# Local and global attention with a gated feed-forward: 224 own key columns a block, probabilities normalised in place

## Chip, core and metric

The kernel runs on one core of a Trainium2 chip. The metric is device time in microseconds, the median of several runs. TensorE (PE in the profile) multiplies, and its weight loads (PEld) overlap the multiplication; VectorE is DVE, ScalarE is ACT, GpSimd is POOL, and SyncE (SP) issues the DMAs. SBUF is the memory on the chip, PSUM the banks that PE writes.

## What is computed

For 8 batches of 8 heads with 512 local and 32 global tokens of 64 features each:

```python
# global queries see every key
out_g = softmax(scale * q_g @ [k_g, k_l].T) @ [v_g, v_l]
# local queries see the global keys, and local keys at most 32 away
s_ll = where(abs(pos_q - pos_k) <= 32, scale * q_l @ k_l.T, -1e9)
out_l = softmax([scale * q_l @ k_g.T, s_ll]) @ [v_g, v_l]
x = [out_g, out_l] with the heads side by side     # 4352 rows of 512
out = (sigmoid(x @ w_gate) * (x @ w_val)) @ w_out   # 512 -> 1536 -> 512
```

The weights come as float64 words and all else as float32.

## The kernel before

**Precision.** A product of float32 numbers is made of float32r parts: a high part (the cast) and a low part (the number less the cast), and three products of them. So operands are split in two: ACT casts and POOL or DVE subtracts. A few heads at the start ("native") use plain float32 instead.

**Attention.** For each head the host lays q, keys and global q side by side in one row block (64 x QK, the 64 features on the partitions). The keys are a run of blocks of 160 columns (BLK): for each block j of 128 queries, a window of 224 columns (WIN) starts at column 160 j, and it holds 32 keys to the left, the first 64 own keys, the 32 global keys, the last 64 own keys and 32 to the right. Neighbouring windows share 64 columns. `load_qk` (L156) loads the row block twice, to the upper and the lower half of the partitions (`qk_raw`). `split_qk` (L187) makes `qk_hi` by a cast of all 1248 columns on ACT (L193), `kl` by a subtract of the 704 key columns on POOL (L194), and the low parts of q by two small subtracts on POOL (L196). `split_v` does the same for v: `vhl`, a cast (L205) and a subtract of 512 columns on POOL (L206).

`local_unit` (L216) treats two blocks of queries, so a head has two such units, in four stages:
- scores in `bank_x` (L225); per block, DVE adds the mask and finds the maximum into `s_sb` (L237, which the order tables call ISA), ACT takes the exponential in place and the sum (L240);
- DVE adds a small number to the sums and inverts them (L243, L244), and `scaled` (L209) multiplies the probabilities: per block one instruction for the 128 own keys (two groups of 64) and one for the 96 others (three groups of 32), from `s_sb` to `p_buf`, in the order of v's rows;
- PE transposes the four 128x128 pieces of `p_buf` into `bank_y` (L254); ACT casts them and DVE subtracts (L264) into `pt`;
- PE multiplies with v (L280, L281), ACT, DVE (L284) and POOL (L285) add the parts.

`global_unit` (L287) does the like for the 32 global queries of a head: four 256-column matmuls of scores (L299: two groups of own keys, each in high and low) and two of 32 columns (L301), a maximum (L304 to L306), an exponential (L308, L309), one scale of 32x576 in place in `pg_buf` (by `scaled`, so L213 too), five transposes (L317), and the product (L330).

**Feed-forward.** `ffn_stream` runs over chunks of 512 tokens and 12 blocks of the hidden dimension: 12 matmuls into `bank_g`, 12 into `bank_v` (L362), and, one block later, 12 of the output into `bank_o` (L396). Between them stand, for the gate, ACT (L370, L376, L377), DVE (L375 and L378, with two inputs in SBUF) and then DVE's product with the values (L380), a cast on ACT (L382) and a subtract on POOL (L383).

**Order.** Attention of the next chunk is issued between groups of four matmuls of the present one, by a table of ticks: a unit every PER = 4 ticks, its four stages 3 ticks apart, loads 16 ticks ahead, splits of q and k 10 and of v 4 ticks ahead. The framework's scheduler then sets each engine's order. Chunks 0 and 1 are half chunks of the first batch and run native, with the conversion of the weights beside them (`convert`, DVE L128 to L136, ACT L132 and L137, POOL L138); the first four heads of chunk 2 are native as well. That is the start-up, about 200 us; up to about 260 us follows the rest of chunk 2's attention, and then six whole chunks of about 139 us, all split. Which engine scales is set by the table NORM: ACT takes two of three in chunk 1 and every second one in chunk 2's native heads, DVE all others.

Of the kernel before, what the change touches and what calls it, by code (L numbers as in the profile page):

```python
# [8 lines left out]
F32 = mybir.dt.float32  # L9
# [8 lines left out]
P = 128  # L18
# [3 lines left out]
NH = 8  # L22
BLK = 160
KEXT = 4 * BLK + 64
K0 = 256
# [3 lines left out]
VS = (2, 3, 6, 7)  # L29
WIN = 224  # L30
DM = 512

# Where work is issued, in ticks of the feed-forward (one tick is four 512-token
# matmuls). Attention units of a chunk follow each other every PER ticks; a unit's
# stages lie STAGES apart, its operands are loaded and split ahead of it.
BASE, PER = 3, 4
STAGES = (0, 3, 6, 9)
LOAD_QK, LOAD_V, SPLIT_QK, SPLIT_V = 16, 9, 10, 4
LOAD_V_NATIVE = 4
# from the first of these ticks of a chunk on, attention is put off by the second  # L40
HOLE = (8, 1)
START = dict(per0=4, base1=1, per1=1.1, base2=23, per2=3, x2=28, lead=8, native_heads=4)
# [12 lines left out]
def kernel(ctx, tc, qk, v, w_gate, w_val, w_out, out_l, out_g):  # L55
# [14 lines left out]

# [1 line left out]
    ident = const.tile([P, P], F32, name="ident")  # L72
# [3 lines left out]
    nc.gpsimd.memset(masks[:, 1], 0.0)  # L76
    # window column c < 96 stands for key c - 32, c >= 128 for key c - 64
    # (relative to the block's first query); the columns between are global
    mid = masks[:, 1]
    for c0, lo, hi in ((0, 0, 64), (128, 96, -32)):  # L80
        cols = mid[:, c0:c0 + 96]
        nc.gpsimd.affine_select(out=cols, in_=cols, pattern=[[1, 96]], compare_op=ALU.is_ge, fill=NEG, base=lo,
                                channel_multiplier=-1)
        nc.gpsimd.affine_select(out=cols, in_=cols, pattern=[[-1, 96]], compare_op=ALU.is_ge, fill=NEG, base=hi,
                                channel_multiplier=1)
    for m, c0 in ((0, 0), (2, 192)):
        nc.scalar.copy(masks[:, m], mid)
        nc.gpsimd.memset(masks[:, m, c0:c0 + 32], NEG)

    p_bufs = [const.tile([P, 2, 256], F32, name="p_buf"),  # L90
              ffn.tile([P, 512], F32, name="p_first", tag="mn", bufs=1).rearrange("p (a c) -> p a c", a=2)]
    nc.vector.memset(p_bufs[0], 0.0)
    nc.vector.memset(p_bufs[1][:, :, WIN:], 0.0)
    pg = const.tile([32, 5 * P], F32, name="pg_buf")
    nc.vector.memset(pg, 0.0)
    xg32 = const.tile([P, KT, NG], F32, name="xg32")

# [53 lines left out]

# [1 line left out]
    def qcol(j):  # L153
# [62 lines left out]
    def local_unit(T, blocks, x32s, h, col0):  # L216
# [4 lines left out]
        for i, j in enumerate(blocks):  # L221
            qj = ks[0][:, qcol(j) - q0:qcol(j) - q0 + P]
            for t, (kt, k0) in enumerate(zip(ks, k0s)):
                js = slice(k0 + j * BLK, k0 + j * BLK + WIN)
                nc.tensor.matmul(s_ps[:, i, 0:WIN], qj, kt[:, js], start=t == 0, stop=t == last)  # L225
# [19 lines left out]
        for i in range(2):  # L245
            main = s_sb[:, i, 32:224].rearrange("p (a c) -> p a c", c=96)[:, :, 0:64]
            scaled(nat, pb[:, i, 0:128].rearrange("p (a c) -> p a c", c=64), main, r[:, i:i + 1])
            side = s_sb[:, i].rearrange("p (a c) -> p a c", c=32)[:, 0:7:3]
            scaled(nat, pb[:, i, 128:224].rearrange("p (a c) -> p a c", c=32), side, r[:, i:i + 1])
        yield  # L250
        pt_ps = ps.tile([P, 4, P], F32, name="bank_y", tag="att", bufs=4)
        for i in range(2):
            for t in range(2):
                nc.tensor.transpose(pt_ps[:, 2 * i + t], pb[:, i, t * P:(t + 1) * P], ident)  # L254
        if nat:
# [31 lines left out]
    def global_unit(T, b, h):  # L287
# [6 lines left out]
        sb = ps.tile([32, 32], F32, name="bank_y", tag="att", bufs=4)  # L294
        for half in range(2):
            o0 = 96 * half
            for t, (src, k0) in enumerate(zip(ks, k0s)):
                view = src[:, k0 + 32:k0 + 32 + 4 * BLK].rearrange("p (j c) -> p j c", c=BLK)[:, :, o0:o0 + 64]
                nc.tensor.matmul(sa[:, :, 64 * half:64 * half + 64], qg, view, start=t == 0, stop=t == last)  # L299
        for t, (src, k0) in enumerate(zip(ks, k0s)):  # L300
            nc.tensor.matmul(sb, qg, src[:, k0 + 96:k0 + 128], start=t == 0, stop=t == last)  # L301
        mg = small.tile([32, 4], F32, name="mg")
# [5 lines left out]
        nc.scalar.activation(pg[:, 0:512], saf, AF.Exp, bias=mg[:, 2:3], scale=0.125, accum_out=sg[:, 0:1])  # L308
# [3 lines left out]
        nc.vector.reciprocal(mg[:, 3:4], mg[:, 3:4])
        scaled(0, pg[:, 0:576], pg[:, 0:576], mg[:, 3:4])
        yield
# [23 lines left out]

# [1 line left out]
    hl_q = []  # L340
# [67 lines left out]

    # ---- driver: attention of the next chunk runs between the matmul groups
    def att_events(ci, start, per, tail=0):  # L410
        """(tick, order, thunk) of all attention work for chunk ci."""
        b, blocks, with_g = chunks[ci]
# [98 lines left out]
def host_layout(inputs):  # L511
# [11 lines left out]
    for j in range(4):  # L523
        o = 32 + j * BLK
        ke[:, o:o + 64] = kl[:, j * P:j * P + 64]
        ke[:, o + 64:o + 96] = kg
        ke[:, o + 96:o + 160] = kl[:, j * P + 64:(j + 1) * P]
# [36 lines left out]
```

## Time and profile before

| what | us |
| --- | --- |
| median of 3 runs | 1267.04 (1265.67 to 1270.59) |
| profiled execution: its span | 1265.6 |
| PE busy | 1221.5 |
| DVE busy | 877.6 |
| ACT busy | 783.3 |
| POOL busy | 570.6 |

The page gives no other time of the profiled execution than its span, from the first instruction to the last; it lies 1.4 us under the median of the runs. In the views, L254 is line 254 of the kernel before, a name like `bank_y` is a tile, x443 is a count, and an arrow names the tile read or the instruction that ended a wait.

### The profile page before, as it was taken

To read this page: it belongs to the slowest core of one execution; us is meant where nothing else is said; L and a number is where in the kernel's file an instruction comes from. 1 tells how busy PE (TensorE), PEld (TensorE's weight loads), DVE (VectorE), ACT (ScalarE), POOL (GpSimd) and SP (SyncE) were. 2 spreads that over 40 slices of the span, in tenths; PEclk is the share of its full clock that TensorE was granted. 3 is DMA by queue.
4 is the path that set the end of the run, shared out by engine and by line. 5 is a ranking of instruction groups with operands and counts; after the bars stand their busy time and mean duration, and the time that the engine had idled before them with its cause. 6 is when DMAs were issued, how large, how long until landed. Compare 5 with 4: busy or idle time off the path is not lost.

```text
span 1265.6 us, 20474 instructions
## 1 busy us (share of the span) xinstructions
PE 1221.5 (97%) x6820; PEld 994.1 (79%) x6820; DVE 877.6 (69%) x2433; ACT 783.3 (62%) x1899; POOL 570.6 (45%) x573
## 2 busy tenths in 40 slices
PE   5899989999999999999999999999999999999998
PEld 4676768788788877888788877888788877888897
DVE  4797976757877777857876778767775787632232
ACT  4586766756666666666666667756765766532233
POOL 1444554545555355545555455535554555311111
PEclk9698999999999999999999999999999999999999
DMA  5576864333333333333333423343334332122143
GB/s 198 197 259 225 254 191 145 92 121 99 92 107 98 115 99 108 91 121 108 107 92 107 126 78 107 109 127 111 92 86 126 116 92 87 44 90 67 67 133 117
DMA packets 59497, 151.90 MB, mean 120 GB/s; under 512 B 6144, under 2 KB 19456, under 8 KB 59392
## 3 DMA queue, kind: packets, MB, share of 16 engines
q1 hardware_dynamic: 59392, 150.59, 38.9%
q8 instruction: 54, 0.88, 0.3%
q14 instruction: 51, 0.42, 0.1%
HBM read 135.36 MB, written 15.20 MB: 119 GB/s over the span
## 4 chain that ended last, share of the span: by engine, by line
PE 77%; DVE 13%; ACT 5%; issue 3%; POOL 1%; DMA 1%; SPq 0%; POOLq 0%; DVEq 0%; ACTq 0%
PE bank_g L362 20%; PE bank_v L362 19%; PE bank_o L396 19%; PE bank_x L225 5%; PE bank_y L254 4%; DVE p_buf L213 3%; DVE th L378 2%; PE bank_y L317 2%; PE bank_x L330 2%; PE bank_x L280 2%; PE bank_x L299 2%; PE bank_x L281 1%; DVE pg_buf L213 1%; ACT s_sb L240 1%; DVE pt L264 1%
## 5 line engine op out<-in xcount | busy, mean ns | idle before, releaser
L362 PE MATMUL bank_g<-xt,wg 128*128 128x512 f32 (+1 forms) x1440 | 340.3, 371 | 1.8 <-DVE th L380 1.8
L362 PE MATMUL bank_v<-xt,wv 128*128 128x512 f32 (+1 forms) x1440 | 332.6, 368 | 3.0 <-DVE pt L264 2.7
L396 PE MATMUL bank_o<-wo,hh 128*128 128x512 f32 x1224 | 334.0, 404 | 0.8 <-ACT hh L382 0.4
L362 PEld LDWEIGHTS bank_g<-xt,wg 128*128 128x128 f32 x1440 | 238.6, 192 | 41.6 <-issue 3.4
L362 PEld LDWEIGHTS bank_v<-xt,wv 128*128 128x128 f32 x1440 | 237.8, 190 | 40.7 <-PE bank_y L301 3.1
L396 PEld LDWEIGHTS bank_o<-wo,hh 128*128 128x128 f32 x1224 | 214.1, 189 | 38.9 <-ACT hh L382 1.2
L383 POOL TENSOR_TENSOR hh<-th,hh 128x512 fp32r<-128x512 f32 (+1 forms) x120 | 137.6, 1147 | 199.7 <-ACT hh L382 198.8
L240 ACT ACTIVATE s_sb<-s_sb,nm 128x224 f32<-128x224 f32 x240 | 113.8, 475 | 143.1 <-DVE nm L237 142.0
L213 DVE TENSOR_SCALAR p_buf<-s_sb,r 128x128 f32<-128x128 f32 (+1 forms) x443 | 151.8, 386 | 4.2 <-PE bank_y L254 0.4
L375 DVE TENSOR_SCALAR mn<-bank_g 128x512 f32<-128x512 f32 (+1 forms) x108 | 67.3, 623 | 110.7 <-ACT th L370 109.3
L378 DVE SCALAR_TENSOR_TENSOR th<-th,mn 128x512 f32<-128x512 f32 (+1 forms) x120 | 101.5, 846 | 59.0 <-ACT mn L376 52.7
L285 POOL TENSOR_TENSOR x<-t 64x256 f32<-64x256 f32 x104 | 76.4, 734 | 142.8 <-DVE t L284 138.7
L194 POOL TENSOR_TENSOR kl<-qk_raw,qk_hi 128x704 fp32r<-128x704 f32 x52 | 88.4, 1701 | 114.8 <-ACT qk_hi L193 114.8
L370 ACT ACTIVATE th<-bank_g 128x512 f32<-128x512 f32 (+1 forms) x120 | 63.5, 529 | 97.7 <-PE bank_g L362 96.1
L382 ACT CAST hh<-th 128x512 fp32r<-128x512 f32 (+1 forms) x120 | 66.5, 554 | 68.1 <-DVE th L380 67.3
L237 DVE CUSTOM_DVE_ANT_0 s_sb<-bank_x,masks 128x224 f32<-128x224 f32 x240 | 83.8, 381 | 12.7 <-PE bank_x L225 8.4
L254 PE MATMUL bank_y<-ident,p_buf 128*128 128x128 f32 x496 | 80.1, 282 | 10.8 <-DVE p_buf L213 6.6
L196 POOL TENSOR_TENSOR qk_hi<-qk_raw,qk_hi 64x256 fp32r<-64x256 f32 x104 | 87.7, 863 | 4.1
L254 PEld LDWEIGHTS bank_y<-ident,p_buf 128*128 128x128 f32 x496 | 60.9, 143 | 32.5 <-ACT pg_buf L308 6.6
L243 DVE TENSOR_SCALAR r<-sm 128x2 f32<-128x2 f32 x128 | 29.3, 229 | 75.5 <-ACT s_sb L240 74.2
L193 ACT CAST qk_hi<-qk_raw 128x1248 fp32r<-128x1248 f32 x52 | 64.1, 1233 | 22.2 <-PE bank_y L301 22.1
L380 DVE TENSOR_TENSOR th<-bank_v,th 128x512 f32<-128x512 f32 (+1 forms) x120 | 72.4, 604 | 5.1 <-PE bank_v L362 1.3
(109 smaller groups left out, 1985.9 us busy)
## 6 DMA issues: line engine op xcount, KB each, us to landing
wo<-wo_dram SPq DMA_DIRECT2D x116, 512.0 KB, 3.5
qk_raw<-in_qk_dram SPq DMA_DIRECT2D x104, 312.0 KB, 4.4
v_raw<-in_v_dram SPq DMA_DIRECT2D x52, 256.0 KB, 2.6
out_dram<-ob SPq DMA_DIRECT2D x34, 256.0 KB, 3.0
xt<-in_w_gate_dram SPq DMA_DIRECT2D x12, 512.0 KB, 4.5
xt<-in_w_val_dram SPq DMA_DIRECT2D x12, 512.0 KB, 4.4
xt<-in_w_out_dram SPq DMA_DIRECT2D x12, 512.0 KB, 4.9
v_nat<-in_v_dram SPq DMA_DIRECT2D x8, 512.0 KB, 5.5
```

Of the source, the lines that this page charges most:

```text
L194: nc.gpsimd.tensor_tensor(kl, t[:, K0:Q1], hi[:, K0:Q1].bitcast(F32), op=ALU.subtract)
L196: nc.gpsimd.tensor_tensor(hi[64:128, r], t[64:128, r], hi[64:128, r].bitcast(F32), op=ALU.subtract)
L213: nc.vector.tensor_scalar(out, in_, by, None, op0=ALU.mult)
L237: anchor[0] = nc.vector.tensor_tensor_reduce(out=s_sb[:, i], in0=s_ps[:, i, 0:WIN], in1=masks[:, m], scale=-0.125, scalar=3.0e38, op0=ALU. ...
L240: nc.scalar.activation(s_sb[:, i], s_sb[:, i], AF.Exp, bias=nm[:, i:i + 1], scale=-1.0, accum_out=sm[:, i:i + 1])
L254: nc.tensor.transpose(pt_ps[:, 2 * i + t], pb[:, i, t * P:(t + 1) * P], ident)
L285: nc.gpsimd.tensor_tensor(dst, t0[:, :, 0], t0[:, :, 1], op=ALU.add)
L362: nc.tensor.matmul(acc, w[a][:, t, fs], xt[:, c, t, x0:x0 + ntok], start=n == 0, stop=n == 11)
L378: nc.vector.scalar_tensor_tensor(th, th, 1.0, mn, op0=ALU.add, op1=ALU.mult)
L380: nc.vector.tensor_tensor(th, acc, th, op=ALU.mult)
L383: nc.gpsimd.tensor_tensor(hh[:, 1, 0:ntok], th, hh[:, 0, 0:ntok].bitcast(F32), op=ALU.subtract)
L396: nc.tensor.matmul(o_ps[t], ph[:, a, t * P:(t + 1) * P], pwo[:, c], start=f2 == 0 and i == 0, stop=f2 == NF - 1 and i == 2)
```

## The change

Each key block now has 224 columns of its own, 128 own keys first, then 32 to the left, 32 global ones and 32 to the right; windows share nothing. A row block grows from 1248 to 1440 columns, the keys in it from 704 to 896. The two scales of a block become one 128x224 scale in place in `s_sb`, which gets two buffers; `p_buf`, `p_first` and their memsets go. The transposes read `s_sb` directly: columns 0 to 127, and 96 to 223, whose first 32 rows meet rows of zeros in v, where the side keys' rows move down by 32. The global queries' own keys are one view of four groups of 128, so two 512-column matmuls do what four did; the scale there is 32x608. The masks are made by other selects. A smaller scratch for DMA descriptors is asked for, which frees SBUF and adds no instruction. Line numbers fall by 4 to 13 (the scale L213 is L207, the transposes of L254 are L242 and L243, L264 is L253).

```diff
-BLK = 160
-KEXT = 4 * BLK + 64
+WIN = 224
+KEXT = 4 * WIN
+GC = 4 * P + 64
...
-    for c0, lo, hi in ((0, 0, 64), (128, 96, -32)):
...
+    for c0, n, step, base in ((0, P, 1, 32), (0, P, -1, 32), (P, 32, 1, 0), (192, 32, -1, -96)):
...
-    p_bufs = [const.tile([P, 2, 256], F32, name="p_buf"),
-              ffn.tile([P, 512], F32, name="p_first", tag="mn", bufs=1).rearrange("p (a c) -> p a c", a=2)]
-    nc.vector.memset(p_bufs[0], 0.0)
-    nc.vector.memset(p_bufs[1][:, :, WIN:], 0.0)
...
-                js = slice(k0 + j * BLK, k0 + j * BLK + WIN)
+                js = slice(k0 + j * WIN, k0 + (j + 1) * WIN)
                 nc.tensor.matmul(s_ps[:, i, 0:WIN], qj, kt[:, js], start=t == 0, stop=t == last)
...
-            s_sb = att.tile([P, 2, WIN], F32, name="s_sb", bufs=1)
+            s_sb = att.tile([P, 2, WIN], F32, name="s_sb", bufs=2)
...
         for i in range(2):
-            main = s_sb[:, i, 32:224].rearrange("p (a c) -> p a c", c=96)[:, :, 0:64]
-            scaled(nat, pb[:, i, 0:128].rearrange("p (a c) -> p a c", c=64), main, r[:, i:i + 1])
-            side = s_sb[:, i].rearrange("p (a c) -> p a c", c=32)[:, 0:7:3]
-            scaled(nat, pb[:, i, 128:224].rearrange("p (a c) -> p a c", c=32), side, r[:, i:i + 1])
+            scaled(nat, s_sb[:, i], s_sb[:, i], r[:, i:i + 1])
         yield
         pt_ps = ps.tile([P, 4, P], F32, name="bank_y", tag="att", bufs=4)
         for i in range(2):
-            for t in range(2):
-                nc.tensor.transpose(pt_ps[:, 2 * i + t], pb[:, i, t * P:(t + 1) * P], ident)
+            nc.tensor.transpose(pt_ps[:, 2 * i], s_sb[:, i, 0:P], ident)
+            nc.tensor.transpose(pt_ps[:, 2 * i + 1], s_sb[:, i, WIN - P:WIN], ident)
...
-        for half in range(2):
-            o0 = 96 * half
-            for t, (src, k0) in enumerate(zip(ks, k0s)):
-                view = src[:, k0 + 32:k0 + 32 + 4 * BLK].rearrange("p (j c) -> p j c", c=BLK)[:, :, o0:o0 + 64]
-                nc.tensor.matmul(sa[:, :, 64 * half:64 * half + 64], qg, view, start=t == 0, stop=t == last)
         for t, (src, k0) in enumerate(zip(ks, k0s)):
-            nc.tensor.matmul(sb, qg, src[:, k0 + 96:k0 + 128], start=t == 0, stop=t == last)
+            view = src[:, k0:k0 + KEXT].rearrange("p (j c) -> p j c", c=WIN)[:, :, 0:P]
+            nc.tensor.matmul(sa, qg, view, start=t == 0, stop=t == last)
+        for t, (src, k0) in enumerate(zip(ks, k0s)):
+            nc.tensor.matmul(sb, qg, src[:, k0 + 160:k0 + 192], start=t == 0, stop=t == last)
...
-        scaled(0, pg[:, 0:576], pg[:, 0:576], mg[:, 3:4])
+        scaled(0, pg[:, 0:GC + 32], pg[:, 0:GC + 32], mg[:, 3:4])
...
-    nc = bacc.Bacc("TRN2", target_bir_lowering=False, num_devices=1)
+    nc = bacc.Bacc("TRN2", target_bir_lowering=False, num_devices=1, dynamic_dma_scratch_size=1024)
```

The order of PE, ACT and POOL is the same from chunk 3 on; within the start-up, instructions trade places locally. Two places on DVE, which PE waits for. The first is the norm of chunk 2's first unit, in the start-up, at 132.7 us of the trace before. Before (L128 to L136 convert weights, where `xt` lends its space; L243 and L244 make the inverse, L213 scales):

```order
L380 TENSOR_TENSOR th<-bank_v,th 128x256
L135 SCALAR_TENSOR_TENSOR xt<-xt 128x512
L243 TENSOR_SCALAR r<-sm 128x2
L136 SCALAR_TENSOR_TENSOR xt<-xt 128x512
L244 RECIPROCAL r<-r 128x2
L128 TENSOR_SCALAR xt<-xt 128x512
L213 TENSOR_SCALAR p_buf<-s_sb,r 128x128 x2
L134 TENSOR_SCALAR xt<-xt 128x512
```

After, the same unit (L367 is what L380 was, L235 and L236 the inverse, L207 the scale, L122 and L129 conversions):

```order
L367 TENSOR_TENSOR th<-bank_v,th 128x256
L235 TENSOR_SCALAR r<-sm 128x2
L236 RECIPROCAL r<-r 128x2
L207 TENSOR_SCALAR s_sb<-s_sb,r 128x224
L122 TENSOR_SCALAR xt<-xt 128x512
L129 SCALAR_TENSOR_TENSOR xt<-xt 128x512
```

Three conversions that stood among the inverse and the scale now stand ahead of or behind them, and DVE has one scale where it had two (ACT does the others).

The second place is a unit of a whole chunk whose scales come shortly before a head's global scores (L304 is their maximum); in the trace before it is at 643 us. Before, from the inverse to the end of that unit:

```order
L244 RECIPROCAL r<-r 128x2
L336 TENSOR_TENSOR y<-bank_x,y 64x64
L213 TENSOR_SCALAR p_buf<-s_sb,r 128x128
L213 TENSOR_SCALAR p_buf<-s_sb,r 128x96
L213 TENSOR_SCALAR p_buf<-s_sb,r 128x128
L213 TENSOR_SCALAR p_buf<-s_sb,r 128x96
L264 TENSOR_TENSOR pt<-bank_y,pt 128x512
L304 TENSOR_REDUCE mg<-bank_x 32x1
L375 TENSOR_SCALAR mn<-bank_g 128x512
L305 TENSOR_REDUCE mg<-bank_y 32x1
L306 TENSOR_SCALAR mg<-mg 32x1
L378 SCALAR_TENSOR_TENSOR th<-th,mn 128x512
```

After, the same place (L253 is L264, L291 is L304, L362 is L375, L365 is L378):

```order
L236 RECIPROCAL r<-r 128x2
L323 TENSOR_TENSOR y<-bank_x,y 64x64
L207 TENSOR_SCALAR s_sb<-s_sb,r 128x224 x2
L253 TENSOR_TENSOR pt<-bank_y,pt 128x512
L291 TENSOR_REDUCE mg<-bank_x 32x1
L362 TENSOR_SCALAR mn<-bank_g 128x512
L292 TENSOR_REDUCE mg<-bank_y 32x1
L293 TENSOR_SCALAR mg<-mg 32x1
L365 SCALAR_TENSOR_TENSOR th<-th,mn 128x512
```

Two scales stand where four stood; nothing else moved there.

More of the change, by code (lines that the diff above doesn't have):

```diff
@@ L29 @@
 VS = (2, 3, 6, 7)
-WIN = 224
 DM = 512
@@ L79 @@
     mid = masks[:, 1]
-    for c0, lo, hi in ((0, 0, 64), (128, 96, -32)):
[L81 to L86, printed above, removed]
+    for c0, n, step, base in ((0, P, 1, 32), (0, P, -1, 32), (P, 32, 1, 0), (192, 32, -1, -96)):
+        cols = mid[:, c0:c0 + n]
+        nc.gpsimd.affine_select(out=cols, in_=cols, pattern=[[step, n]], compare_op=ALU.is_ge, fill=NEG, base=base,
+                                channel_multiplier=-step)
+    for m, c0 in ((0, P), (2, 192)):
         nc.scalar.copy(masks[:, m], mid)
         nc.gpsimd.memset(masks[:, m, c0:c0 + 32], NEG)
-    p_bufs = [const.tile([P, 2, 256], F32, name="p_buf"),
-              ffn.tile([P, 512], F32, name="p_first", tag="mn", bufs=1).rearrange("p (a c) -> p a c", a=2)]
-    nc.vector.memset(p_bufs[0], 0.0)
-    nc.vector.memset(p_bufs[1][:, :, WIN:], 0.0)
     pg = const.tile([32, 5 * P], F32, name="pg_buf")
@@ L101 @@
     wo_dram = [dram.tile([P, 2, DM], F32, name=f"wo_dram{f}") for f in range(NF)]
-    cnt = {"p": 0, "norm": 1}
+    cnt = {"norm": 1}
     conv_bufs = []
@@ L232, in local_unit @@
         r = small.tile([P, 2], F32, name="r")
-        pb = p_bufs[cnt["p"] % 2 if T["first"] else 0]
-        cnt["p"] += 1
         for i, j in enumerate(blocks):
@@ L308, in global_unit @@
         nc.scalar.activation(pg[:, 0:512], saf, AF.Exp, bias=mg[:, 2:3], scale=0.125, accum_out=sg[:, 0:1])
-        nc.scalar.activation(pg[:, 544:576], sb, AF.Exp, bias=mg[:, 2:3], scale=0.125, accum_out=sg[:, 1:2])
+        nc.scalar.activation(pg[:, GC:GC + 32], sb, AF.Exp, bias=mg[:, 2:3], scale=0.125, accum_out=sg[:, 1:2])
         yield
@@ L418, in att_events @@
         c0 = 0 if blocks[0] == 0 else K0
-        c1 = QK if blocks[-1] == 3 else K0 + BLK + WIN
+        c1 = QK if blocks[-1] == 3 else K0 + 2 * WIN
         heads, group = [], {}
@@ L523, in host_layout @@
     for j in range(4):
[L524 to L527, printed above, removed]
+        o = j * WIN
+        ke[:, o:o + P] = kl[:, j * P:(j + 1) * P]
+        if j > 0:
+            ke[:, o + P:o + P + 32] = kl[:, j * P - 32:j * P]
+        ke[:, o + P + 32:o + P + 64] = kg
+        if j < 3:
+            ke[:, o + P + 64:o + WIN] = kl[:, (j + 1) * P:(j + 1) * P + 32]
         ve[:, VM[j]] = vl[:, j * P:(j + 1) * P]
         if j > 0:
-            ve[:, VS[j], 0:32] = vl[:, j * P - 32:j * P]
-        ve[:, VS[j], 32:64] = vg
+            ve[:, VS[j], 32:64] = vl[:, j * P - 32:j * P]
+        ve[:, VS[j], 64:96] = vg
         if j < 3:
-            ve[:, VS[j], 64:96] = vl[:, (j + 1) * P:(j + 1) * P + 32]
+            ve[:, VS[j], 96:P] = vl[:, (j + 1) * P:(j + 1) * P + 32]
     ql = q_l.reshape(N, SL, D)
```

## The prediction

> **What bounds the kernel now.** I read the engines' busy time first, then the chain that ended last, then busy time by stage, then the places where TensorE stands still.
>
> ```profile
> PE 1221.5 (97%) x6820; PEld 994.1 (79%) x6820; DVE 877.6 (69%) x2433; ACT 783.3 (62%) x1899; POOL 570.6 (45%) x573
> ...
> PE 77%; DVE 13%; ACT 5%; issue 3%; POOL 1%; DMA 1%; SPq 0%; POOLq 0%; DVEq 0%; ACTq 0%
> PE bank_g L362 20%; PE bank_v L362 19%; PE bank_o L396 19%; PE bank_x L225 5%; PE bank_y L254 4%; DVE p_buf L213 3%; DVE th L378 2%; PE bank_y L317 2%; PE bank_x L330 2%; PE bank_x L280 2%; PE bank_x L299 2%; PE bank_x L281 1%; DVE pg_buf L213 1%; ACT s_sb L240 1%; DVE pt L264 1%
> ```
>
> PE is busy 97% and carries 77% of the chain; the normalisation (L213, p_buf) carries 3%. The stages differ. The columns of the next rows are the stretch, then busy time and count for PE, PEld, DVE, ACT and POOL, then PE's clock, DMA share and GB/s:
>
> ```profile
> 130.00:165.00 35.00, 32.88 (x215) 26.01 (x216) 33.75 (x87) 26.50 (x75) 18.31 (x13) 1.00 0.82 261
> ...
> 600.00:800.00 200.00, 197.27 (x1081) 160.25 (x1080) 153.28 (x434) 133.03 (x311) 104.89 (x107) 1.00 0.36 104
> ```
>
> In the start-up, where weights are converted, DVE is the full engine (33.75 of 35 us). In the steady part PE has 197.27 of 200, DVE 153.28 and POOL 104.89. A shorter DVE instruction gains time there only where PE stands waiting for DVE, so the change is worth what those places are worth.
>
> **The norms.** The groups of the instructions that go, and below them the shortest, median and longest of one (columns of the first four: count | busy us, mean ns):
>
> ```profile
> L213 DVE TENSOR_SCALAR p_buf<-s_sb,r 128x128 f32<-128x128 f32 x222 | 104.3, 471 | 4.0 <-PE bank_y L254 0.2
> L213 DVE TENSOR_SCALAR p_buf<-s_sb,r 128x96 f32<-128x96 f32 x221 | 66.0, 300 | 0.3 <-PE bank_y L254 0.2
> L211 ACT ACTIVATE p_buf<-s_sb,r 128x128 f32<-128x128 f32 x18 | 6.6, 393 | 1.2 <-DVE r L244 1.2
> L211 ACT ACTIVATE p_buf<-s_sb,r 128x96 f32<-128x96 f32 x19 | 6.4, 366 | 0.4 <-DVE r L244 0.4
> ```
>
> ```profile
> L213 DVE TENSOR_SCALAR p_buf<-s_sb,r x443: 265/297/1387, 58.2 to 1093.6; 128x128 f32<-128x128 f32 x74, 128x96 f32<-128x96 f32 x74
> L213 DVE TENSOR_SCALAR pg_buf<-pg_buf,mg x64: 498/899/1670, 61.5 to 1097.4; 32x576 f32<-32x576 f32 x64
> ```
>
> The 96-column form costs 300, always; the 128-column form costs 265 alone, and its mean of 471 is waiting. The 32x576 scale, contiguous and in place, costs 498 alone. So columns in a plain row cost (498 - 265)/(576 - 128) = 0.52 ns each, and 128x224 in place should take 265 + 96 x 0.52 = 315 ns alone. [...] I take 315, because the contiguous 576 row is its nearest kind. Four norms of a unit are 1130 ns of durations, two are 630; they overlap by some tens of ns at each seam, so a unit's norms end about 0.4 us sooner where POOL does not interfere. On ACT 393 + 366 = 759 becomes about 366 + 128 x 27/32 = 474.
>
> [...]
>
> **Start-up, 0 to 200 us: -4.** What TensorE waits for the norms there, from the waits of that stretch (us, times, longest):
>
> ```profile
> PE bank_y L254 <- DVE p_buf L213: 6.6, 5, 2.7
> ...
> PE bank_y L254 <- DVE p_first L213: 1.8, 2, 1.3
> ```
>
> That is 8.4 us. Unblocked, the norms shrink from 1130 to 630 ns a unit, 44%: 0.44 x 8.4 = 3.7. The two memsets and the other mask selects stand at the very start, under the first load (last part), and count nothing. The blocked part stays:
>
> ```profile
> 132.75 1.26 DVE p_buf L213
> ```
>
> This piece of the chain is a norm held while POOL splits a weight, and a 224 norm can be held likewise. Against this, reciprocal and norm now stand next to each other where a conversion stood between (front part, first place), and the conversion behind them starts later. I take -4; ends: -8.4 (all waiting goes) and +2.5 (two more instructions held as long as this one, where the order is new).
>
> **Half chunk, 200 to 260 us: -1.5.** Here L280 waits for L264, which follows the norms on DVE:
>
> ```profile
> PE bank_x L280 <- DVE pt L264: 2.9, 4, 1.0
> ```
>
> Four waits, each shortened by up to 0.4: -1.5. Ends: -2.9 and 0.
>
> **Six whole chunks: +4.8.** The stored row grows from 1248 to 1440 columns and POOL's subtract from 704 to 896:
>
> ```profile
> L193 ACT CAST qk_hi<-qk_raw 128x1248 fp32r<-128x1248 f32 x52 | 64.1, 1233 | 22.2 <-PE bank_y L301 22.1
> L205 ACT CAST vhl<-v_raw 128x512 fp32r<-128x512 f32 x52 | 32.0, 615 | 0.0
> ...
> L194 POOL TENSOR_TENSOR kl<-qk_raw,qk_hi 128x704 fp32r<-128x704 f32 x52 | 88.4, 1701 | 114.8 <-ACT qk_hi L193 114.8
> L206 POOL TENSOR_TENSOR vhl<-v_raw,vhl 128x512 fp32r<-128x512 f32 x52 | 67.7, 1301 | 8.4 <-ACT vhl L205 6.0
> ```
>
> ACT: (1233 - 615)/736 = 0.84 ns a column, 192 more are +0.16 us. POOL: (1701 - 1301)/192 = 2.08 ns, 192 more are +0.40. So kl ends 0.56 to 0.6 us later in each of 52 heads. Who waits for it? Not the scores, which come much later, but a DVE instruction with two SBUF inputs that happens to start while POOL runs. One chunk's first place, in order (start, duration):
>
> ```profile
> 597.14 1.22 ACT L193 CAST qk_hi<-qk_raw 128x1248 fp32r<-128x1248 f32 x1
> ...
> 598.44 1.71 POOL L194 TENSOR_TENSOR kl<-qk_raw,qk_hi 128x704 fp32r<-128x704 f32 x1 [2.06 <-ACT qk_hi L193]
> 598.99 1.70 DVE L378 SCALAR_TENSOR_TENSOR th<-th,mn 128x512 f32<-128x512 f32 x1 [0.99 <-ACT mn L376]
> ...
> 602.01 0.67 DVE L264 TENSOR_TENSOR pt<-bank_y,pt 128x512 fp32r<-128x512 f32 x1
> ...
> 602.74 0.38 PE L280 MATMUL bank_x<-pt,vhl 128*128 128x256 f32 x1 [0.16 <-DVE mg L312]
> ```
>
> L378 takes 1.70 and ends 0.54 after kl. Behind it on DVE are L311, L380, L284 and L264, in that order before and almost so after, and 0.06 us after L264 ends (602.68) PE starts L280. This chain has no slack: +0.6. A second place, 49 us on:
>
> ```profile
> 647.42 1.71 POOL L194 TENSOR_TENSOR kl<-qk_raw,qk_hi 128x704 fp32r<-128x704 f32 x1 [2.65 <-ACT qk_hi L193]
> ...
> 647.98 1.70 DVE L378 SCALAR_TENSOR_TENSOR th<-th,mn 128x512 f32<-128x512 f32 x1 [0.78 <-ACT mn L376]
> ...
> 650.99 0.67 DVE L264 TENSOR_TENSOR pt<-bank_y,pt 128x512 fp32r<-128x512 f32 x1
> ...
> 651.92 0.28 PE L280 MATMUL bank_x<-pt,vhl 128*128 128x256 f32 x1
> ```
>
> L264 ends 651.66, L280 could start at 651.72 and starts at 651.92: 0.2 of slack, so +0.4. Ahead of this second place the change gains something:
>
> ```profile
> 643.13 1.95 DVE L213 TENSOR_SCALAR p_buf<-s_sb,r 128x128 f32<-128x128 f32 x4
> ...
> 643.49 1.28 POOL L206 TENSOR_TENSOR vhl<-v_raw,vhl 128x512 fp32r<-128x512 f32 x1
> ...
> 645.00 0.67 DVE L264 TENSOR_TENSOR pt<-bank_y,pt 128x512 fp32r<-128x512 f32 x1
> ...
> 645.82 1.87 PE L362 MATMUL bank_v<-xt,wv 128*128 128x512 f32 x7 [0.44 <-DVE pt L264]
> ```
>
> The third of four norms met vhl. With two, the second starts about 0.25 after the first, at 643.38, ahead of vhl at 643.49; POOL would wait instead, L264 come over 1 us sooner and PE's 0.44 go. But L280 at 651.92 then hangs on the kl chain, which starts from ACT's cast and not from PE, so the 0.44 is given back there; the +0.4 stands whether or not it goes. A like place, 16 us earlier:
>
> ```profile
> 627.58 1.89 DVE L213 TENSOR_SCALAR p_buf<-s_sb,r 128x128 f32<-128x128 f32 x4
> ...
> 631.85 0.42 PEld L254 LDWEIGHTS bank_y<-ident,p_buf 128*128 128x128 f32 x4 [0.48 <-ACT pg_buf L308]
> ```
>
> Here PE waits for a bank that ACT frees after work behind those norms; of the 0.48 I count -0.2. A chunk: 0.6 + 0.4 - 0.2 = +0.8, six are +4.8. Ends: -5 (both stalls gone, 0.44 + 0.4 each, kl without effect) and +11 (each chunk one more L378 caught, 1.0 by its 1.70 against the 0.67 of L264 with as many columns).
>
> [...]
>
> **What costs nothing.**
>
> ```profile
> 644.70 0.28 PE L299 MATMUL bank_x<-qk_hi 128*32 128x256 f32 x1
> ...
> 645.05 0.28 PE L299 MATMUL bank_x<-kl,qk_hi 128*32 128x256 f32 x1
> ...
> 650.98 1.10 PE L396 MATMUL bank_o<-wo,hh 128*128 128x512 f32 x4
> ```
>
> Global scores: four 256-column matmuls start 0.117 apart (0.35/3); 512-column ones 0.23 to 0.24 apart (1.10 less a last duration of 0.40, over 3). Two for four: 0.47 either way. The transposes keep shape and count. s_sb is now held until its transposes, but there are two of it, and the unit before the last has long been transposed when the next scores are masked; a single buffer would hold DVE up there.
>
> ```profile
> qk_raw<-in_qk_dram SPq DMA_DIRECT2D x104, 312.0 KB, 4.4
> ...
> ACT qk_hi L193 <- PE bank_y L301: 22.1, 28, 1.1
> ...
> PE bank_x L225 <- DMA qk_nat<-in_qk_dram: 9.1, 1, 9.1
> ```
>
> Loads are 15% larger, so about 0.7 longer by the 4.4; the cast waits for PE's release of its output buffer, 28 times, and not for the load, which covers it; without cover each would cost up to 0.7 at the cast. [...]
>
> **Sum.** -4 - 1.5 + 4.8 + 0.3 = -0.4. The profiled span of 1265.6 lies 1.4 under the median of 1267.04; against the median this gives 1266.6.
>
> **Rivals.**
> - *Faster.* DVE's time in the start-up is worth its whole waiting (-8.4), the half chunk -2.9, and kl hits L378 no harder than now because L378 or ACT's cast shifts: -11, about 1256. For: DVE at 96% there. Against: the held norm at 132.75, and the rows of L378, which starts half a us behind kl at both places.
> - *Slower.* POOL's longer kl holds one further L378 in each chunk, wherever L378 starts less than 0.6 us after a kl now ends: +6 on top of the +4.8, with start-up gain as forecast: 1266.6 + 6 = 1272.6; with the start-up gain eaten by conversions that trade places, 1276. It decides from one extra capture a chunk.
> [...]
>
> **Chances.** Under 0.5% (6.3 us) a measurement of this kernel hardly tells a change from none. My forecast 0.5 with its own range 1261 to 1272, the slow form 0.05 (both same); faster rival 0.26; slower rival 0.19. The range for all reaches from 1256 to 1275.
>
> **What the new profile should show.** Norms 128x224 with a shortest of about 315; kl at 2.1 us; cast 1.39; L378 behind kl at about 1.7 to 2.3, and PE's wait at the first place about 0.6 longer in each chunk; the wait before L362 at the third place gone; L254's waits for norms before 200 us down from 8.4 to about 5. I am wrong if the period of the chunks does not grow, if the start-up ends later than now, or if kl gets caught behind norms often enough that the scores wait.

## The result, and the profile after

The changed kernel takes 1285.3 us (median of 4 runs, 1283.96 to 1288.23) against 1267.11 before (now four runs): a ratio of 1.014, with an interval of 1.0115 to 1.0166. I had forecast 1266.6 and a range up to 1275. The change makes the kernel 18 us slower.

Where the time went can be read without any wait: both kernels run the same 4104 feed-forward matmuls in the same order, so the start of the n-th of them is a clock. How much later than before it starts in the changed kernel (us, from the two traces):

```
n-th matmul                396     684    3276    last
starts before at         198.7   267.9  1098.5  1260.7
later in the changed one  +4.8    +3.3   +16.4   +16.4
```

So the start-up loses 4.8, the half chunk gains 1.5, the six whole chunks lose 13.1 and the tail loses nothing. The forecast had -4, -1.5 and +4.8 for the three. These are the two profiled executions, whose spans differ by 16.3 (1281.9 against 1265.6); the medians differ by 18.2.

Of the page after, busy time and chain:

```profile
PE 1226.0 (96%) x6692; PEld 982.2 (77%) x6692; DVE 847.1 (66%) x2196; ACT 784.5 (61%) x1878; POOL 594.9 (46%) x573
...
PE 61%; DVE 20%; ACT 10%; issue 5%; DMA 2%; POOL 1%; SPq 0%; DVEq 0%; POOLq 0%; ACTq 0%
```

DVE has 30 us less to do, as intended, and yet its share of the chain grew from 13% to 20%; PE's fell from 77% to 61%. The steady stretch shown before (columns as there):

```profile
600.00:800.00 200.00, 195.01 (x1043) 155.25 (x1042) 142.67 (x371) 133.37 (x308) 108.09 (x103) 1.00 0.38 107
```

DVE is 10 us less busy in it and PE 2.3 us less: TensorE waits more for an engine that has less to do. The list of waits tells for which instructions. PE's waits for pt (us, times, longest), from the trace after:

```profile
PE bank_x L269 <- DVE pt L253: 18.3, 32, 0.9
```

L253 and L269 are what L264 and L280 were. From the trace before, the same wait:

```profile
PE bank_x L280 <- DVE pt L264: 6.5, 13, 1.0
```

It grew by 11.8 us. The instructions of the change and those that it touches (by form, then shortest, median and longest):

```profile
L207 DVE TENSOR_SCALAR s_sb<-s_sb,r 128x224 f32<-128x224 f32 x224 | 97.8, 453 | 3.0
L365 DVE SCALAR_TENSOR_TENSOR th<-th,mn 128x512 f32<-128x512 f32 x84 | 87.1, 1037 | 63.3 <-ACT mn L363 63.3
...
L207 DVE TENSOR_SCALAR pg_buf<-pg_buf,mg 32x608 f32<-32x608 f32 x64 | 68.4, 1069 | 1.9
```

```profile
L207 DVE TENSOR_SCALAR s_sb<-s_sb,r x224: 315/336/1457, 56.0 to 1108.4; 128x224 f32<-128x224 f32 x112
L207 DVE TENSOR_SCALAR pg_buf<-pg_buf,mg x64: 515/1129/1680, 59.5 to 1113.8; 32x608 f32<-32x608 f32 x64
```

The new norm takes 315 ns alone, as forecast. The scale of pg_buf, which gained 32 columns, costs 515 alone but 1069 in the mean: it is held, and more than before (883).

The first place of the prediction, in the trace after (start, duration, and in brackets the idle time before):

```profile
605.10 1.38 ACT L187 CAST qk_hi<-qk_raw 128x1440 fp32r<-128x1440 f32 x1
...
606.55 2.11 POOL L188 TENSOR_TENSOR kl<-qk_raw,qk_hi 128x896 fp32r<-128x896 f32 x1 [1.90 <-ACT qk_hi L187]
607.11 2.11 DVE L365 SCALAR_TENSOR_TENSOR th<-th,mn 128x512 f32<-128x512 f32 x1 [1.17 <-ACT mn L363]
...
610.65 0.67 DVE L253 TENSOR_TENSOR pt<-bank_y,pt 128x512 fp32r<-128x512 f32 x1
...
611.37 0.39 PE L269 MATMUL bank_x<-pt,vhl 128*128 128x256 f32 x1 [0.90 <-DVE pt L253]
```

Cast 1.38, kl 2.11, L365 held until kl ends, PE waiting 0.90 where it waited 0.16: the forecast chain, at the forecast size. What the forecast does not have stands 16 us further on:

```profile
622.96 2.12 POOL L188 TENSOR_TENSOR kl<-qk_raw,qk_hi 128x896 fp32r<-128x896 f32 x1 [2.12 <-ACT qk_hi L187]
...
625.03 1.29 POOL L370 TENSOR_TENSOR hh<-th,hh 128x512 fp32r<-128x512 f32 x1
625.05 1.60 DVE L207 TENSOR_SCALAR pg_buf<-pg_buf,mg 32x608 f32<-32x608 f32 x1
...
627.18 0.67 DVE L253 TENSOR_TENSOR pt<-bank_y,pt 128x512 fp32r<-128x512 f32 x1
...
627.90 0.38 PE L269 MATMUL bank_x<-pt,vhl 128*128 128x256 f32 x1 [0.36 <-DVE pt L253]
```

The same place before:

```profile
614.16 1.71 POOL L194 TENSOR_TENSOR kl<-qk_raw,qk_hi 128x704 fp32r<-128x704 f32 x1 [1.09 <-ACT qk_hi L193]
...
615.83 1.28 POOL L383 TENSOR_TENSOR hh<-th,hh 128x512 fp32r<-128x512 f32 x1
...
617.27 0.97 DVE L213 TENSOR_SCALAR pg_buf<-pg_buf,mg 32x576 f32<-32x576 f32 x1
...
618.77 0.67 DVE L264 TENSOR_TENSOR pt<-bank_y,pt 128x512 fp32r<-128x512 f32 x1
```

hh (L383, now L370) stands behind kl in POOL's queue. Before, hh ended 0.16 ahead of the scale of pg_buf (617.11 and 617.27), and the scale's 0.97 came from a shorter POOL instruction behind it (0.74, L196). With kl 0.4 longer and started later by the longer cast, hh now starts with the scale and is waited for to its end; the scale takes 1.60, and the pt behind it on DVE comes late for PE, which waits 0.36. There are three such places in each chunk. At the other two hh already ran into the scale before and now does so longer: the scale takes 1.36 instead of 1.12 (576 us) and 1.48 instead of 0.92 (674 us), and PE waits 0.26 and 0.32 behind it.

The start-up: PE's waits for the norms there grew instead of shrinking (before 6.6 and 1.8):

```profile
PE bank_y L242 <- DVE s_first L207: 6.1, 4, 2.7
...
PE bank_y L242 <- DVE s_sb L207: 5.5, 4, 3.2
```

### The profile page after: what moved, and what is told of

Its sections match the earlier page's. It is cut to its first block, busy times and chain, and to the rows that moved or that the text cites. A ratio compares the mean times of both kernels' runs of the same rounds, so it can differ in the third digit from the quotient of the medians.

```text
span 1281.9 us, 19816 instructions
## 1 busy us (share of the span) xinstructions
PE 1226.0 (96%) x6692; PEld 982.2 (77%) x6692; DVE 847.1 (66%) x2196; ACT 784.5 (61%) x1878; POOL 594.9 (46%) x573
## 4 chain that ended last, share of the span: by engine, by line
PE 61%; DVE 20%; ACT 10%; issue 5%; DMA 2%; POOL 1%; SPq 0%; DVEq 0%; POOLq 0%; ACTq 0%
PE bank_g L349 17%; PE bank_o L383 15%; PE bank_v L349 14%; DVE th L365 4%; PE bank_x L219 4%; DVE pg_buf L207 3%; DVE th L367 2%; ACT s_sb L232 2%; DVE t L273 2%; ACT qk_hi L187 2%; PE bank_x L317 2%; ACT mn L363 2%; PE bank_x L269 2%; PE bank_y L242 2%; PE bank_y L304 2%
## 5 line engine op out<-in xcount | busy, mean ns | idle before, releaser
L383 PE MATMUL bank_o<-wo,hh 128*128 128x512 f32 x1224 | 335.5, 404 | 0.7 <-ACT hh L369 0.4
L383 PEld LDWEIGHTS bank_o<-wo,hh 128*128 128x128 f32 x1224 | 214.4, 189 | 38.2 <-ACT hh L369 1.2
L370 POOL TENSOR_TENSOR hh<-th,hh 128x512 fp32r<-128x512 f32 (+1 forms) x120 | 140.5, 1170 | 188.7 <-ACT hh L369 187.6
L188 POOL TENSOR_TENSOR kl<-qk_raw,qk_hi 128x896 fp32r<-128x896 f32 x52 | 110.0, 2116 | 135.9 <-ACT qk_hi L187 135.9
L365 DVE SCALAR_TENSOR_TENSOR th<-th,mn 128x512 f32<-128x512 f32 (+1 forms) x120 | 107.8, 899 | 78.3 <-ACT mn L363 72.2
L362 DVE TENSOR_SCALAR mn<-bank_g 128x512 f32<-128x512 f32 (+1 forms) x108 | 67.0, 620 | 111.6 <-ACT th L357 111.6
L207 DVE TENSOR_SCALAR s_sb<-s_sb,r 128x224 f32<-128x224 f32 x224 | 97.8, 453 | 3.0
L229 DVE CUSTOM_DVE_ANT_0 s_sb<-bank_x,masks 128x224 f32<-128x224 f32 x240 | 83.2, 380 | 16.4 <-PE bank_x L219 16.1
L187 ACT CAST qk_hi<-qk_raw 128x1440 fp32r<-128x1440 f32 x52 | 72.6, 1396 | 32.7 <-PE bank_y L288 32.5
L235 DVE TENSOR_SCALAR r<-sm 128x2 f32<-128x2 f32 x128 | 33.2, 259 | 76.7 <-ACT s_sb L232 73.9
L367 DVE TENSOR_TENSOR th<-bank_v,th 128x512 f32<-128x512 f32 (+1 forms) x120 | 72.5, 604 | 7.0 <-PE bank_v L349 1.4
L269 PE MATMUL bank_x<-pt,vhl 128*128 128x256 f32 x208 | 57.7, 300 | 18.3 <-DVE pt L253 18.3
L253 DVE TENSOR_TENSOR pt<-bank_y,pt 128x512 fp32r<-128x512 f32 x104 | 70.1, 674 | 4.3 <-ACT pt L252 4.3
```

The costliest lines, as they stand in the source:

```text
L187: nc.scalar.copy(hi, t)
L188: nc.gpsimd.tensor_tensor(kl, t[:, K0:Q1], hi[:, K0:Q1].bitcast(F32), op=ALU.subtract)
L207: nc.vector.tensor_scalar(out, in_, by, None, op0=ALU.mult)
L229: anchor[0] = nc.vector.tensor_tensor_reduce(out=s_sb[:, i], in0=s_ps[:, i, 0:WIN], in1=masks[:, m], scale=-0.125, scalar=3.0e38, op0=ALU. ...
L269: nc.tensor.matmul(o_ps[:, i], vt[:, VM[j], :], pt[:, :, 2 * i, :], start=True, stop=False)
L365: nc.vector.scalar_tensor_tensor(th, th, 1.0, mn, op0=ALU.add, op1=ALU.mult)
```

## Experiments

Theory A: the wider rows cost the chunks, because POOL's longer kl holds L365, and, by hh queued behind it, the scale of pg_buf. Theory B: the in-place norm and its being held costs them. The table gives the median, the ratio to the kernel before with its interval, and how much later than before the n-th matmul of the profiled execution starts.

```
kernel                              us     ratio (interval)           396    684   3276
changed kernel                  1285.3  1.014  (1.0115 to 1.0166)   +4.8   +3.3  +16.4
before, wide rows only          1286.9  1.0155 (1.0129 to 1.0181)   +5.5   +6.2  +22.3
before, norms only              1262.5  0.9958 (0.9942 to 0.9974)   +2.8   +0.7   -4.4
changed, kl of 704 columns      1272.1  1.0036 (1.0021 to 1.0050)   +7.6   +4.7   +6.2
changed, kl in two              1275.1  1.0063 (1.0041 to 1.0084)   +9.1   +8.1   +9.6
before, kl in two               1256.3  0.9915 (0.9895 to 0.9936)   -1.4   -2.1  -11.0
before, kl, vhl, hh in two      1249.7  0.9863 (0.9842 to 0.9885)   +0.3   -1.8  -16.2
before, long first loads        1268.2  1.0012 (0.9997 to 1.0026)   +0.6   +0.6   +0.6
changed, kl, vhl, hh in two     1266.9  0.9998 (0.9982 to 1.0014)   +4.8   +2.3   -0.7
same, turns of ACT shifted      1264.7  0.9989 (0.9970 to 1.0009)   +2.7   +0.2   -3.9
same, conversions first         1269.1  1.0012 (0.9996 to 1.0027)   +8.1   +6.1   +1.6
```

**Wide rows alone.**

```diff
 # the kernel before
-KEXT = 4 * BLK + 64
+KEXT = 4 * 224
...
```

The lines left out lengthen the loads of the first half chunk to match and ask for the smaller DMA scratch.

> The kernel before, with nothing changed but the length of the rows: 192 columns that nobody reads are loaded, cast on ACT and subtracted on POOL (kl 128x896). Norms, p_buf, transposes and the global scores stay. Theory A (the longer kl on POOL costs the chunks, through L378 held by it and through hh, which is queued behind it on POOL and then holds the scale of pg_buf): a chunk's period grows from 139.1 by 1.8 to 2.6 us, the six chunks by 11 to 16, the time is 1277 to 1285. Theory B (the in-place 128x224 norm, held by POOL, and what hangs on it costs the chunks): the period stays within 0.5 of 139.1 and the time within 4 us of 1267.

Measured: the six chunks lose 16.1 (22.3 - 6.2), 2.7 a chunk, and the time is 1286.9, both a little above what I expected of theory A. Rows that nobody reads to the end cost more than the whole change does there; theory B falls here. It is not the length alone that differs: in the whole chunks one DVE instruction of 0.2 us trades places twice a chunk, and the start-up has an order of its own. The scales that hh holds are also not all the same ones (at 580, 615 and 665 us they take 1.42 to 1.56). PE's wait for pt in this kernel:

```profile
PE bank_x L280 <- DVE pt L264: 17.1, 33, 1.0
```

**Norms alone.**

```diff
 # the kernel before, rows of 1248 columns
-            scaled(nat, pb[:, i, 0:128].rearrange("p (a c) -> p a c", c=64), main, r[:, i:i + 1])
...
-            scaled(nat, pb[:, i, 128:224].rearrange("p (a c) -> p a c", c=32), side, r[:, i:i + 1])
+            scaled(nat, s_sb[:, i], s_sb[:, i], r[:, i:i + 1])
...
-                nc.tensor.transpose(pt_ps[:, 2 * i + t], pb[:, i, t * P:(t + 1) * P], ident)
+            nc.tensor.transpose(pt_ps[:, 2 * i], s_sb[:, i, 0:P], ident)
+            nc.tensor.transpose(pt_ps[:, 2 * i + 1], s_sb[:, i, WIN - P:WIN], ident)
```

> The kernel before with the norms alone changed: one 128x224 scale a block in place in two s_sb buffers, transposes of its columns 0 to 127 and 96 to 223, no p_buf; rows stay 1248 long, global scores are four matmuls. The rows of v are not rearranged, so probabilities meet other rows than in the reference. Theory A: the period is 139.1 or up to 1 us less (the stall ahead of L362 at the fourth norm goes, kl is as short as before), and what the start-up does follows its own order of instructions: 1258 to 1272. Theory B: the period is 141 or more, and the time 1278 or more.

Measured: the six chunks gain 5.1, the start-up loses 2.8. The part of the change that was meant to help does help, by 0.42% in all. Wide rows and norms by themselves give +16.1 and -5.1 in the chunks, together +11.0; the change itself gives +13.1, and the 2.1 between them have no cause here.

**A shorter kl in the changed kernel.**

```diff
-        nc.gpsimd.tensor_tensor(kl, t[:, K0:Q1], hi[:, K0:Q1].bitcast(F32), op=ALU.subtract)
+        nc.gpsimd.tensor_tensor(kl, t[:, K0:K0 + 704], hi[:, K0:K0 + 704].bitcast(F32), op=ALU.subtract)
...
```

> The changed kernel with POOL's subtract cut from 896 to 704 columns and nothing else (same order on every engine); the low parts of the keys are then read from other columns, so the scores' low parts are not the reference's. Theory A: the period falls from 141.4 to 138.5 to 139.5, the six chunks by 11 to 17, the start-up stays 4.8 us later than before at 200 us, time 1268 to 1274. Theory B: nothing changes, 1285 within 3.

Measured: the chunks' loss falls from 13.1 to 1.5, with every instruction in the same place on every engine. 192 columns of one POOL instruction are 11.6 us of the 18. The start-up stands at +7.6 here, not at +4.8 as in the changed kernel with the same order; the last experiments come back to that. PE's wait for pt:

```profile
PE bank_x L269 <- DVE pt L253: 8.5, 17, 1.0
```

**kl in two halves in the changed kernel.**

```diff
+        for a in (0, KEXT // 2):
+            c = slice(K0 + a, K0 + a + KEXT // 2)
+            nc.gpsimd.tensor_tensor(kl[:, a:a + KEXT // 2], t[:, c], hi[:, c].bitcast(F32), op=ALU.subtract)
```

> The changed kernel with POOL's subtract in two instructions of 448 columns (same order otherwise; about 0.24 us more POOL time a head). Theory A, if a held DVE instruction gets through between the two halves: the stall of 1.07 us before L280 (now L269) at the first and third place falls below 0.5, the places where pg_buf meets hh grow by up to 0.24, the period falls by about 1 us to 140.4 and the time to 1279. Theory A, if POOL's next instruction goes first: the period grows by 0.3 to 0.7, time 1287 to 1290. Theory B: within 3 of 1285.

Measured: 1275.1, better than either branch. The chunks lose 1.4 instead of 13.1. The first place, with all the work of the changed kernel and 0.25 us more of kl on POOL a head (122.9 us in all 52 against 110.0):

```profile
607.61 2.71 POOL L190 TENSOR_TENSOR kl<-qk_raw,qk_hi 128x448 fp32r<-128x448 f32 x2 [1.91 <-ACT qk_hi L187]
608.17 1.15 DVE L367 SCALAR_TENSOR_TENSOR th<-th,mn 128x512 f32<-128x512 f32 x1 [1.17 <-ACT mn L365]
...
611.47 0.39 PE L271 MATMUL bank_x<-pt,vhl 128*128 128x256 f32 x1
```

The held DVE instruction takes 1.15 where it took 2.11: it goes ahead between the halves. PE's wait of 0.90 is gone. What cost here was not POOL's time but the length of its single instructions. I had expected the places of pg_buf and hh to get worse by 0.24. Instead one of the three got much better: at 624.89 the scale now starts 0.15 ahead of hh, which the split made later, so the scale takes 0.52 and hh waits (1.53). The other two scales take 1.34 and 1.08 (1.36 and 1.48 in the changed kernel); over the whole run the mean is 879 ns against 1069. PE's waits for pt are 5.6 us in the whole run.

**The same in the kernel before: kl alone, then kl, vhl and hh.** The edits are the loop above with halves of 352 columns, and

```diff
+        for a in (0, 4):
+            nc.gpsimd.tensor_tensor(vhl[:, a:a + 4, D:2 * D], t[:, a:a + 4], vhl[:, a:a + 4, 0:D].bitcast(F32), op=ALU.subtract)
...
+                        for a in range(0, ntok, 256):
+                            e = min(a + 256, ntok)
+                            nc.gpsimd.tensor_tensor(hh[:, 1, a:e], th[:, a:e], hh[:, 0, a:e].bitcast(F32), op=ALU.subtract)
```

> The kernel before with POOL's kl in two instructions of 352 columns, all else in the same order. Theory A (a DVE instruction that needs what POOL holds is let through as soon as one POOL instruction ends): L378 at the first and third place takes about 1.1 us instead of 1.70, the stall of 0.33 us at the first place goes, and the period falls by 0.3 to 0.6 us: 1263 to 1266. Theory C (splitting gained in the changed kernel for another reason, such as hh coming at another moment): L378 stays at 1.7 or more, and the 0.24 us more of POOL's time make it 1267 to 1270.

Measured: 1256.3. L378 (now L380) takes 0.95 at the first place:

```profile
593.56 2.31 POOL L196 TENSOR_TENSOR kl<-qk_raw,qk_hi 128x352 fp32r<-128x352 f32 x2 [2.01 <-ACT qk_hi L193]
594.11 0.95 DVE L380 SCALAR_TENSOR_TENSOR th<-th,mn 128x512 f32<-128x512 f32 x1 [0.99 <-ACT mn L378]
```

The gain is well over twice what I expected of theory A: 1263 to 1266 was the range, and a period shrinks by 1.5 us and not by 0.3 to 0.6. PE's wait at a place where vhl holds L378 goes too, though vhl is as long as before; why is not shown.

> The kernel before with POOL's kl, vhl and hh (whole chunks) in two instructions each, all else in the same order. Theory A: also the norms and the L378 held by vhl and the scales of pg_buf held by hh get through half way: of the 2.2 us of stalls in a period 1.2 to 1.8 go, and 1 to 3 us in the half chunk after 200 us: 1254 to 1261. Theory C: 1267 or more.

Measured: 1249.7, below the expected range, and 17 us below the kernel before. In the whole chunks TensorE hardly stands still any more:

```profile
600.00:800.00 200.00, 200.00 (x1109) 165.17 (x1108) 149.44 (x439) 136.18 (x319) 114.43 (x148) 1.00 0.37 105
```

PE's wait for pt and the chain of this kernel:

```profile
PE bank_x L283 <- DVE pt L267: 1.1, 3, 0.5
```

```profile
PE 89%; DVE 6%; ACT 2%; issue 2%; DMA 1%; POOL 0%; SPq 0%; POOLq 0%; DVEq 0%; ACTq 0%
```

POOL works 37 us longer here than before (607.3 against 570.6), in 188 instructions more, and the kernel is 1.4% faster. This is the version that beats both kernels.

**The three splits in the changed kernel.** The same edits.

> The changed kernel with kl, vhl and hh of POOL in two instructions each. Theory A: on top of what the split of kl gave (1275), the scales of pg_buf held by hh get through: 0.3 to 1 us a period less, 1268 to 1273. Theory C: 1275 or more, by the 0.24 us of each further POOL instruction.

Measured: 1266.9, below the expected 1268 to 1273. With the holds cut short the change comes out level with the kernel before, and 17 us behind the kernel before with the same splits. Its chunks gain 3.0 over before, its start-up still loses 4.8. Between the two split kernels the chunks differ by 11.4 (-14.4 against -3.0). The matmuls' own waits for pt hardly show this (1.7 us in the whole run), but the loads of pt as weights (PEld) do: they wait 12.7 us for it, against 3.4 in the kernel before with the splits. So pt is still late in the wide rows' kernel; which instruction makes it late was not followed up, and that even half of the longer kl does it is argued, not shown.

**The start-up: loads or order.** The loads of the first two chunks made as long as in the changed kernel:

```diff
+                e = (0, 64, 192, 0)[T["native"]]
+                ce = slice(c.start, c.stop + e)
-                nc.sync.dma_start(t[:, 0:c.stop - c.start], qk[n:n + 2, :, c].rearrange("n p c -> (n p) c"))
+                nc.sync.dma_start(t[:, 0:c.stop - c.start + e], qk[n:n + 2, :, ce].rearrange("n p c -> (n p) c"))
...
```

> The kernel before with the loads of chunks 0 and 1 alone as long as in the changed kernel (704 and 1184 columns instead of 640 and 992; the surplus is not used). Theory S1 (the start-up loses by the longer loads, which the weights' loads share the DMA engines with): at 200 us it is 3 to 6 us later than before, 1270 to 1273. Theory S2 (it loses by the order of conversions, norms and scales on DVE and POOL): within 1.5 us of before, 1266 to 1268.5.

Measured: +0.6 at 200 us and 1268.2, where S1 expected 1270 or more. These loads are at most a small part (those of chunk 2's native heads were left as they were, and from 132 us on a few instructions trade places). Then, on the changed kernel with the splits, only the order:

```diff
-NORM = {0: "v", 1: "v", 2: "ssv", 3: "sv"}
+NORM = {0: "v", 1: "v", 2: "vss", 3: "sv"}
```

> The changed kernel with kl, vhl and hh in two instructions each, and in the start-up the turns of ACT and VectorE at the scales of chunk 1 shifted by one (vss for ssv): same number of instructions on every engine but one or two, in another order up to about 130 us, and in particular fewer waits for PE inside the conversions on VectorE. Theory S2 (the start-up's loss is the order of conversions, norms and waits on VectorE): at 200 us it differs by 2 us or more from the 4.8 us that the changed kernel was late there, likely earlier: 1262 to 1265. Theory S3 (the loss hangs on the amount of work, which is the same): 4 to 6 us late at 200 us, 1266 to 1268.

```diff
-        queue.append((g, 4, lambda f=f: convert_w(f, 0)))
+        queue.append((g, 1, lambda f=f: convert_w(f, 0)))
```

(and the other two conversions of a block likewise)

> The changed kernel with kl, vhl and hh in two instructions each, and the conversions of the weights issued ahead of the attention stages of the same tick instead of behind them: the same instructions in another order up to about 190 us. Theory S2: at 200 us it differs by 2 us or more from 4.8 us late, in either direction: 1260 to 1264 or 1269 and more. Theory S3: 4 to 6 us late, 1266 to 1268.

Measured at 200 us: +2.7 and +8.1 where the same work in the first order had +4.8. The first of the two starts its feed-forward at the same time (47.1 and 47.2 us), is 3.1 us ahead at 128 us (-0.4 against +2.7) and 2.1 ahead at 200; its order differs up to about 180 us, not only up to 130 as I had expected. The second starts its feed-forward 3.5 us later (50.7) and falls no further behind from there than the first order does (7.2 us against 7.4), so it says little.

How much is an execution by itself? The changed kernel and its variants with a short kl, a split kl and the three splits run the same instructions in one order up to 175 us. They start the feed-forward between 47.2 and 52.5 us and stand at +4.8, +7.6, +9.1 and +4.8. The kernel before and its two split variants, in one order too up to 175 us, stand at 0, -1.4 and +0.3. So the loss of the start-up is clear, its size is known to some 4 us only, and the two runs point to the order without settling its share.

## Why the prediction was wrong

**Right.** The norm's price (315 ns forecast, 315 measured), the cast (1.39 and 1.38 us), kl (2.1 and 2.11), L378 held behind kl, the first place (+0.6 forecast, +0.71 between the matmuls on its two sides), the stall ahead of L362 gone and given back at the second place (+0.4 forecast, -0.66 and +1.20 measured), the half chunk (-1.5, -1.5), the global scores, the hidden loads. No run shows the +0.3 of the first load: PE waits 9.0 for it, 9.1 before.

**Chunks: +4.8 forecast, +13.1 measured.** The step that failed is the question "who waits for it?" after kl's price. I answered it with L378 alone. I had said that what is queued behind a longer instruction counts, and did not follow it on POOL's own queue: hh comes behind kl, moves with it, and meets the scale of pg_buf, which held half a microsecond of PE's slack. There are three such places in a chunk. On the clock of the matmuls a chunk loses 0.71 at the first place, +1.20 - 0.66 at the second, and about half a microsecond (0.47 to 0.60) at each of the three new ones. Ahead of the one shown above it gains 0.77, because a wait behind vhl goes there, and the loss that follows may in part give this back. With the smaller steps the chunk comes to +2.2, where +0.8 was forecast. The rows were there: the scale's 883 in the mean against 498 alone said that POOL already held it, and by the trace before 49 of the 64 took over 0.55 us, each ending 0.31 to 0.32 after a POOL instruction. The rival "slower" had the right mechanism at the wrong instruction, one capture a chunk where there were three, and chance 0.19; its own upper figure of 1276 lay outside my range, which ended at 1275. One step of 1.06 us in the profiled execution, at 716 us, is no hold: ACT there waits 1.65 for the store of the output tile `ob` where it waited 0.16 before, and pt comes late behind that. Whether the change delays the store was not measured.

In the rows shown, the DVE instruction that came second waited out the whole POOL instruction: 2.11 behind kl and 1.15 behind half of it, where the median of its group is 0.69.

**Start-up: -4 forecast, +4.8 measured.** The failed step is the 44% taken off PE's waits for norms, 8.4 us. They grew to 11.6. The order at one favourable place was taken for the whole; at others the new order is worse. One of them, before:

```profile
111.89 0.67 DVE L135 SCALAR_TENSOR_TENSOR xt<-xt 128x512 uint32<-128x512 uint32 x1
112.49 0.15 DVE L244 RECIPROCAL r<-r 128x2 f32<-128x2 f32 x1
112.66 0.69 DVE L136 SCALAR_TENSOR_TENSOR xt<-xt 128x512 uint32<-128x512 uint32 x1
```

and after, with SP's load of the next weight block that waits for this conversion:

```profile
112.54 0.69 DVE L129 SCALAR_TENSOR_TENSOR xt<-xt 128x512 uint32<-128x512 uint32 x1
...
116.16 0.42 DVE L362 TENSOR_SCALAR mn<-bank_g 128x256 f32<-128x256 f32 x1 [2.22 <-ACT th L357]
...
117.17 0.68 DVE L130 SCALAR_TENSOR_TENSOR xt<-xt 128x512 uint32<-128x512 uint32 x1
```

```profile
117.88 0.39 SPq L111 DMA_DIRECT2D xt<-in_w_val_dram  x1
```

The last step of the conversion (L130, before L136) now stands behind an instruction that waits 2.22 for ACT, which had itself waited 2.64 for PE, and the conversion ends 4.5 us later than before (117.8 against 113.4). That the start-up's loss is the sum of such places is argued, not shown. A second possible cause stands beside it, which the forecast put at nothing: PE's clock. Between 60 and 200 us the mean granted clock is 0.95 before and 0.90 in the changed kernel, 0.94 in the two split variants of the kernel before and 0.89 to 0.91 in the three variants that share the changed kernel's order. 0.05 of 140 us is 7 us of full clock, as an upper bound on what it cost, since PE also waits in that time; no run separates the clock from the order. Norms alone stand at +2.8 there and wide rows alone at +5.5, each in its own order, while the kernel before and its split variants stand between -1.4 and +0.3.

## What to carry over

When an instruction gets longer, follow every engine's queue behind it, its own first, to the instruction that next meets another engine; here a mean far above the shortest time of a group (883 against 498) named one that was held already. Where the trace shows an instruction of one engine waiting out a whole one of another, as L365 did behind kl (2.11, median 0.69), try cutting the longer one: 37 us more of POOL time in shorter pieces made this kernel 1.4% faster. A planner that reorders a start-up is an unknown of several microseconds, to be kept in the range even where one place looks better: at 200 us every other order tried here is later than that of the kernel before, by 0.6 to 9.1.

## What the runs showed of the hardware

At kl the held DVE instruction went first when POOL's instruction ended, even though POOL had the next half ready: the two halves of kl take 1.84 us where nobody waits and 2.31 where a DVE instruction goes between them.

```profile
608.62 1.84 POOL L196 TENSOR_TENSOR kl<-qk_raw,qk_hi 128x352 fp32r<-128x352 f32 x2 [1.91 <-ACT qk_hi L193]
```

That is of the kernel before with kl in two. It was otherwise at a place where the DVE instruction started only 0.11 ahead of the end: in the kernel before, a scale of pg_buf starts at 602.78, POOL's instruction ends at 602.89, and the scale still waits out hh behind it and takes 1.67.

PE's granted clock was 0.52 over 3.4 us (81.40 to 84.80), some 3 us after PE had stood still for 1.09 (up to 78.54); in the changed kernel, where the scale of pg_buf stood behind a conversion that POOL held (L128, 1.27 where it takes 0.41 alone). The columns are as in the windows above, the clock third from the end:

```profile
76.90:78.50 1.60, 0.55 (x4) 0.23 (x2) 1.60 (x4) 0.96 (x4) 0.77 (x1) 1.00 1.06 394
78.50:81.40 2.90, 2.86 (x24) 2.13 (x25) 2.59 (x8) 1.46 (x5) 0.00 (x0) 0.97 0.33 79
81.40:84.80 3.40, 3.40 (x15) 3.01 (x13) 1.47 (x4) 2.49 (x7) 1.27 (x1) 0.52 0.86 239
```

In the slow stretch the matmuls of 256 columns into `bank_v` start 0.21 apart (82.29, 82.50, 82.71), ahead of it 0.11 to 0.12 apart (80.89, 81.00, 81.12). That the stall brought the drop is not shown, and not every stall has one: in the same kernel PE stands still for 1.43 at 157.4 us, and the clock stays at 1.00 up to 176.
